# Attention and two expert mixtures on one core: the attention's transposed output in groups of 32 rows instead of 96

## The chip, the cores and the metric

The kernel runs on one core of one Trainium2 chip. The metric is the device time of one execution in microseconds (us). A core has five engines with queues of their own: TensorE (PE, with PEld for its weight loads), VectorE (DVE), ScalarE (ACT), GpSimd (POOL) and SyncE (SP), which issues most of the DMAs. All data are computed in float32; a matmul of float32 operands shows in the trace as two passes, each with a weight load (LDWEIGHTS) and a MATMUL record.

## The reference

Three stages follow one another. First a linear attention with decay over 4 batches, 8 heads, 768 positions and 48 dimensions a head:

```python
for t in range(S):
    cur = np.einsum('bhd,bhe->bhde', u[None] * kt, vt)
    y[:, :, t] = np.einsum('bhd,bhde->bhe', rt, state + cur)
    state = wt[:, :, :, None] * state + np.einsum('bhd,bhe->bhde', kt, vt)
```

Its output, heads side by side, is x with 3072 tokens and 384 columns. The first mixture computes h = x @ w_in (384 x 1024), h times its softmax, a layer norm with the gains g_ln, and the product with w_out (1024 x 384). The second mixture takes for each token the expert with the largest logit x @ w_gate, out of 8, and computes gate * (relu(x @ w1[e]) @ w2[e]) with w1[e] of 384 x 1024.

## The kernel before, in words

The attention works on 24 units: 6 chunks of 128 positions times 4 batches. A unit's tensors r, k and w are transposed on TensorE (L693), two heads in one block of 128 rows (64 rows a head, 48 of them used), so that there are four pairs p = 0 to 3. Products of the decays turn r and k into `rt` and `kt`. `scores` (L763 to L768) multiplies them, head by head, into two PSUM banks (4 and 5), with 48 rows of the array from row 0 or from row 64 on. `mask` (L771, VectorE) puts the causal part into `am`, on whose diagonal GpSimd has laid the u term (L748).

`y` (L775 to L781) computes the unit's output already transposed, features on partitions and the 128 positions along the free axis, in bank 4. For pair p, the stationary operand of 96 columns is the state `St[b]` (for chunks after the first; moving operand `rt`), and then v of either head with zeros beside it (`lv` holds 48 columns of v and 48 zeros a head; moving operand `am`). So the bank gets four blocks of 96 rows by 128 positions, from 12 matmuls (8 in the first chunk), with all 128 columns of the array addressed or 96 of them.

The mixture wants three blocks of 128 features for its contraction. `high` (L784 to L788) therefore copies blocks 0 to 2 to rows 0 to 95 in one ScalarE copy (L785) and the fourth block's three thirds to rows 96 to 127 in three more of 32x128 (L787); `low` (L790 to L794) does the same on VectorE with the subtraction that leaves the low part of each number (L791, L793). The two parts are the operands of `moe_h`, which forms each float32 product from three cheaper ones (`mm3`, L183). Since the features then stand in an order of their own, w_in is loaded in that order too: `x_rows` (L217) names two slices of rows for each block, and `from_f64` loads each slice with a DMA of its own (L224 to L226).

Next on the same banks: U (L808 to L811), the product that updates the state, uses bank 4 from chunk steps in the mixture stage on, and the next unit's scores overwrite banks 4 and 5. So both wait for the last of L793.

The order of all work around this is written out by hand: each step is entered in a plan with a nominal time (`at`, tables `OFF`), the steps are sorted by it, and `_ORDER` gives the sequence in which they are issued (`emit`). Every engine works through its steps in that order. Units 0 to 6 run beside the preparation of w_out and w_in (float64 to float32 by bit operations on VectorE, L231 to L237), units 7 to 23 beside one tile each of the first mixture, seven units behind. After the last unit come the rest of the mixture and the experts. `warm` (L1084) issues products that nobody reads, where TensorE has no work early on.

Of the kernel before, what the change touches and what calls it, by code (L numbers as in the profile page):

```python
# [7 lines left out]
F32 = mybir.dt.float32  # L8
# [5 lines left out]
ALU = mybir.AluOpType  # L14
# [17 lines left out]
# Places by number of tokens, in the order in which they are worked on, and the room of each; the last one's rest has a path of its own.  # L32
# [5 lines left out]
# Issue order: position in the issue sequence -> index of the step in the plan sorted by nominal time.  # L38
# [82 lines left out]
def rwkv_moe_kernel(ctx: ExitStack, tc: tile.TileContext, r, k, v, w, u, w_in, w_out, g_ln, w_gate, w1, w2, out, dbg=None):  # L121
# [44 lines left out]
    # sums of the inverse decay products, of the squares of the first mixture, of the decay products: bounds that NaN fails too  # L166
# [16 lines left out]
    def mm3(o, terms):  # L183
        """The products of operands in two parts each, high parts first; the product of both low ones is below float32."""
        n = len(terms)
        for i, (ah, al, bh, bl) in enumerate(terms):
            nc.tensor.matmul(o, ah, bh, start=(i == 0), stop=False)  # L187
            nc.tensor.matmul(o, ah, bl, start=False, stop=False)  # L188
        for i, (ah, al, bh, bl) in enumerate(terms):
            nc.tensor.matmul(o, al, bh, start=False, stop=(i == n - 1))  # L190

    def mm3_steps(o, terms, n):
        """The same in pieces of n products."""
        seq = [(ah, b) for ah, al, bh, bl in terms for b in (bh, bl)] + [(al, bh) for ah, al, bh, bl in terms]
        for i, (a, b) in enumerate(seq):
            nc.tensor.matmul(o, a, b, start=(i == 0), stop=(i == len(seq) - 1))  # L196
            if i % n == n - 1:
                yield
# [5 lines left out]
    # A plan is a list of steps with nominal times; every engine issues its steps in that order.  # L204
# [11 lines left out]
    # The rows of a block of the attention's transpose: those of a pair of heads, and a third of the last pair's.  # L216
    def x_rows(kk):  # L217
        return (slice(0, 96), slice(96 * kk, 96 * kk + 96)), (slice(96, 128), slice(3 * 96 + 32 * kk, 3 * 96 + 32 * kk + 32))

    def from_f64(src, n, pool, ck=None):  # L220
        """float64 to float32 by its bits: sign and exponent and 20 bits of the high word, 3 of the low one.
        Below float32's range it is 0, or, with ck, sums there say that a value was below."""
# [21 lines left out]
    def prep_w_in(c, pool, ck=None):  # L244
        kk, n = divmod(c, 2)
        ns = slice(512 * n, 512 * n + 512)
        a = yield from from_f64([(rows, w_in[at, ns]) for rows, at in x_rows(kk)], 512, pool, ck)
        yield lambda: nc.scalar.copy(out=wih[:, kk, ns], in_=a)
        yield lambda: nc.gpsimd.tensor_tensor(out=wil[:, kk, ns], in0=a, in1=wih[:, kk, ns].bitcast(F32), op=ALU.subtract)
# [7 lines left out]
    def prep_gate(f, st, wgt, pool, tp, gp):  # L257
        """Rows of w_out times the gate's weights, for the logits to come out of the same product as the mixture."""
        def tr():
            for kk in range(KD):  # L260
                nc.tensor.transpose(tp[:, kk, :], st()[:, kk * 128:(kk + 1) * 128], ident)
        yield tr
        wT = pool("wT")[:, 0:DM].rearrange("p (k n) -> p k n", k=KD)
        yield lambda: nc.scalar.copy(out=wT, in_=tp)

        def lg():
            for kk in range(KD):
                nc.tensor.matmul(gp[:, f, :], wT[:, kk, :], wgt[:, kk, :], start=(kk == 0), stop=(kk == KD - 1))
        yield lg
# [43 lines left out]
    def moe_act(u, halves, mw):  # L313
        """halves: the hidden values, as one pattern or as two of one bank each."""
# [121 lines left out]
    def experts_loop(x2d=None, tokd=None):  # L436
        """Every expert over all tokens, the others' results dropped; without those over its sorted rows."""
# [56 lines left out]
    def general_path():  # L494
# [44 lines left out]
        with ExitStack() as gs:  # L539
# [11 lines left out]
            with tc.For_i(0, NTOK, 128) as t0:  # L551
                x = ga2.tile([128, DM], F32, tag="gx", name="gx")
                xk = x.rearrange("p (k n) -> p k n", k=KD)
                nc.sync.dma_start(out=xk[:, :, 0:96], in_=xd[bass.ds(t0, 128), 0:288].rearrange("p (k n) -> p k n", k=KD))
                nc.sync.dma_start(out=xk[:, :, 96:128], in_=xd[bass.ds(t0, 128), 288:384].rearrange("p (k n) -> p k n", k=KD))
# [20 lines left out]
    # the attention's buffers go when its last tile is done, and those of the experts take their room  # L576
# [23 lines left out]
    def xslot(m):  # L600
        """Where the two parts of a tile's transpose wait: in the first weight buffers, as long as no expert has them; one place apart, for the last tile."""
        i = m % 7
        parts = [xs[:, 0], xs[:, 1]] if i == 2 else [t[:, DM * XPOS[i]:DM * XPOS[i] + DM] for t in wa0]
        return [t.rearrange("p (k n) -> p k n", k=KD) for t in parts]
# [12 lines left out]
    def lazy(t, make, gaps):  # L617
        """Steps of a generator that allocates as it goes: each is drawn when its turn comes."""
# [10 lines left out]
    # Nominal times of the steps of a unit from the start of its step: attention with the preparation of  # L629
    # w_out beside it, with that of w_in, with a tile of the mixture, and the mixture alone.  # L630
# [122 lines left out]
    def plan_A(i, t, mode):  # L753
# [5 lines left out]
        yp = bank[4][0:2 * D]  # L759
# [15 lines left out]
        def y():  # L775
            vf = v_.rearrange("p h d -> p (h d)")
            terms = [(p, St[b][:, p, :], u["rt"][:, p, :]) for p in range(4)] if c else []
            terms += [(p, vf[:, 96 * (2 * p + q) - 48 * q:96 * (2 * p + q) - 48 * q + 96], u["am"][:, q, p, :]) for q in range(2) for p in range(4)]
            for n, (p, a, m) in enumerate(terms):
                nc.tensor.matmul(yp[:, p, :], a, m, start=(n == 0), stop=(n == len(terms) - 1), skip_group_check=True)  # L780
# [3 lines left out]
        def high():  # L784
            nc.scalar.copy(out=xh[0:96], in_=yp[:, 0:3, :])  # L785
            for kk in range(KD):
                nc.scalar.copy(out=xh[96:128, kk, :], in_=yp[32 * kk:32 * kk + 32, 3, :])  # L787
        at(o("x"), high)  # L788

        def low():  # L790
            nc.vector.tensor_tensor(out=xl[0:96], in0=yp[:, 0:3, :], in1=xh[0:96].bitcast(F32), op=ALU.subtract)  # L791
            for kk in range(KD):
                nc.vector.tensor_tensor(out=xl[96:128, kk, :], in0=yp[32 * kk:32 * kk + 32, 3, :], in1=xh[96:128, kk, :].bitcast(F32), op=ALU.subtract)  # L793
# [57 lines left out]
    # groups of token tiles that are gated together  # L851
# [44 lines left out]
    def gate_steps(g, bk):  # L896
        """The first of the largest logits' experts, its gate, the row among the sorted tokens, and the way there."""
# [69 lines left out]
    # The first is the one with most of the first tokens, so that its work can start before the last tokens have theirs;  # L967
    # the others follow by their numbers of tokens, as PLACE has it. The j-th has room for SLOTS[j] tokens.
# [90 lines left out]
    # the first loads, then the constant buffers  # L1059
# [8 lines left out]
    def init():  # L1068
# [10 lines left out]
        # each partition's sums start at its share of the expert's first row: ranks come out as rows  # L1079
# [4 lines left out]
    def warm(n):  # L1084
        """The tensor engine's clock rises only under load: products that nobody reads, where there is no work yet."""
# [21 lines left out]
    def scratch(c):  # L1107
        """Where the preparation of a block of weights works: buffers that the mixture uses later."""
# [12 lines left out]
    def named(make, times):  # L1121
        """Steps of a generator at given times."""
# [80 lines left out]
    def check():  # L1203
        """1 for more tokens of the last place, 2 for a place with too little room, 4 for decays or values out of bounds or an expert's rows overrun."""
# [79 lines left out]
    # the first expert's first tokens, beside the end of the first mixture  # L1284
# [18 lines left out]
    # the order of the others  # L1303
# [18 lines left out]
    for j in range(1, NE):  # L1322
        # the weights and tokens of a place are made ready during the one before
# [72 lines left out]
```

## Time and profile before

| | |
|---|---|
| Median of 3 runs | 702.67 us (701.42, 703.84, 702.67) |
| Profiled execution, first to last instruction | 701.8 us |
| What lies around that span | not listed; the runs' median is 0.9 us above it |
| Granted TensorE clock, mean | 0.972 of full speed |
| TensorE, VectorE, ScalarE, GpSimd busy | 93%, 63%, 49%, 50% |
| DMA | 72.45 MB, mean 103 GB/s |

The execution has three parts: to about 101 us the attention's first units and the preparation of weights, to about 383 us attention and mixture together, and then the mixture's end and the experts. Busy shares of the whole span mix these, so the rows below are taken by part. Matmuls are pipelined: a record lasts longer than the engine's turn, so the time of a run of matmuls is read from the start of its first to the start of what follows.

### The profile page before, as it was taken

The page shows a single profiled execution, that of the slowest core. Times are in us where ns is not written, and L with a number is a line of the kernel's source. Part 1 is how long each engine was busy: PE and PEld are TensorE (multiplying, and loading weights), DVE is VectorE, ACT ScalarE, POOL GpSimd, SP SyncE. Part 2 cuts the span into 40 slices and gives each one's busy share as a digit, 9 for nine tenths or more (in the row PEclk, how much of TensorE's full clock was granted, in tenths as well). Part 3 has the DMA queues.
Part 4 walks back from the last instruction along what each step waited for, and adds up shares of the span by engine and source line. Part 5 has one row for each costly group of instructions (what it writes and reads, how often), then busy time and mean ns, then how long its engine had stood idle before and what let it go on. Part 6 is the DMA issues. An engine that isn't in the chain of part 4 may idle for free. (4 is left out here: it accounts for less than half of the span.)

```text
span 701.8 us, 11888 instructions
## 1 busy us (share of the span) xinstructions
PE 650.1 (93%) x4279; PEld 604.1 (86%) x4279; DVE 444.6 (63%) x947; ACT 346.1 (49%) x759; POOL 350.8 (50%) x341
## 2 busy tenths in 40 slices
PE   6787779898999999999989999999999999999993
PEld 6777668887988978998978998999899999999993
DVE  7999999968987888699887779752203121131220
ACT  3677566545553545545643556433535344353430
POOL 5666578344344445344461153326637374667721
PEclk9789799999999999999999999999999999999997
DMA  7856323562611413050200420155444253544400
GB/s 175 210 132 146 95 59 90 170 170 58 147 35 33 104 23 68 23 114 24 57 35 13 154 84 13 57 160 188 149 141 139 91 176 125 182 135 145 157 20 35
DMA packets 125193, 72.45 MB, mean 103 GB/s; under 512 B 104167, under 2 KB 115932, under 8 KB 125125
## 3 DMA queue, kind: packets, MB, share of 16 engines
q1 hardware_dynamic: 121845, 62.13, 33.3%
q0 software_dynamic: 3280, 9.47, 3.6%
q8 instruction: 36, 0.59, 0.4%
q14 instruction: 32, 0.26, 0.1%
HBM read 55.79 MB, written 16.29 MB: 103 GB/s over the span
## 5 line engine op out<-in xcount | busy, mean ns | idle before, releaser
L1257 DVE SCALAR_TENSOR_TENSOR hl<-bank,hh 128x384 fp32r<-128x384 f32 (+5 forms) x70 | 37.6, 552 | 141.4 <-ACT hh L1256 125.8
L1050 POOL TENSOR_TENSOR wbl<-stg,wbh 128x768 fp32r<-128x768 f32 x32 | 58.8, 1852 | 30.0 <-ACT wbh L1049 25.6
L196 PE MATMUL bank<-wbh,hh 128*128 128x384 f32 (+4 forms) x216 | 72.9, 338 | 0.0
L196 PE MATMUL bank<-wbl,hh 128*128 128x384 f32 (+4 forms) x216 | 72.6, 336 | 0.0
L187 PE MATMUL bank<-xth,wah 128*128 128x384 f32 (+5 forms) x210 | 71.2, 345 | 0.5 <-DVE rr L955 0.5
L1050 POOL TENSOR_TENSOR wal<-stg,wah 128x1024 fp32r<-128x1024 f32 x24 | 57.3, 2401 | 28.1 <-ACT wah L1049 28.1
L188 PE MATMUL bank<-xtl,wah 128*128 128x384 f32 (+5 forms) x210 | 69.7, 337 | 0.0
L187 PE MATMUL bank<-wbh,lh 128*128 128x392 f32 x192 | 67.5, 351 | 1.3 <-ACT xo L873 0.8
L1256 ACT ACTIVATE hh<-bank 128x384 fp32r<-128x384 f32 (+5 forms) x70 | 33.6, 490 | 66.6 <-PE bank L190 59.0
L188 PE MATMUL bank<-wbl,lh 128*128 128x392 f32 x192 | 65.5, 341 | 0.0
L748 POOL TENSOR_TENSOR am<-ident,a 128x1024 f32<-128x1024 f32 x24 | 46.7, 1946 | 28.0 <-DVE a L743 19.8
L1276 POOL DMA_INDIRECT out_dram<-yo,xg x28 | 27.6, 984 | 64.6 <-ACT yo L1273 42.7
L726 POOL TENSOR_TENSOR tq<-qe,yq 128x512 f32<-128x512 f32 x24 | 29.7, 1238 | 60.0 <-ACT yq L721 59.9
L780 PE MATMUL bank<-am,lv 128*96 128x128 f32 x384 | 49.3, 284 | 5.7 <-DVE am L771 4.8
L780 PEld LDWEIGHTS bank<-am,lv 128*96 128x96 f32 x384 | 45.9, 171 | 6.7 <-DVE am L771 3.2
L823 POOL TENSOR_TENSOR St<-su,qe 64x192 f32<-64x192 f32 x40 | 24.8, 621 | 48.0 <-DVE su L818 36.4
L190 PE MATMUL bank<-xth,wal 128*128 128x384 f32 (+5 forms) x210 | 48.2, 337 | 0.0
L961 POOL DMA_INDIRECT xsd<-xo,ai x24 | 25.4, 1057 | 35.0 <-DMA xsd<-xo,ai 14.1
L187 PE MATMUL pair<-wah,wah 128*128 128x512 f32 x102 | 42.1, 413 | 0.0
L196 PE MATMUL bank<-wbh,hl 128*128 128x384 f32 (+4 forms) x216 | 42.1, 336 | 0.0
L187 PEld LDWEIGHTS bank<-xth,wah 128*128 128x128 f32 x210 | 39.5, 188 | 2.3 <-DVE rr L955 0.7
L188 PEld LDWEIGHTS bank<-xtl,wah 128*128 128x128 f32 x210 | 39.5, 188 | 1.3
(241 smaller groups left out, 1753.0 us busy)
## 6 DMA issues: line engine op xcount, KB each, us to landing
stg<-in_moe_w_dram SPq DMA_DIRECT2D x32, 384.0 KB, 4.5
stg<-in_moe_w_dram SPq DMA_DIRECT2D x24, 512.0 KB, 4.5
xsd<-zrow SPq DMA_DIRECT2D x16, 386.0 KB, 3.8
xg<-xsd SPq DMA_DIRECT2D x24, 193.0 KB, 2.7
lw<-in_w_dram SPq DMA_DIRECT2D x24, 192.0 KB, 3.3
lr<-in_r_dram SPq DMA_DIRECT2D x24, 192.0 KB, 4.2
lk<-in_k_dram SPq DMA_DIRECT2D x24, 192.0 KB, 3.8
lv<-in_v_dram SPq DMA_DIRECT2D x24, 192.0 KB, 3.1
```

The costliest lines, as they stand in the source:

```text
L187: nc.tensor.matmul(o, ah, bh, start=(i == 0), stop=False)
L188: nc.tensor.matmul(o, ah, bl, start=False, stop=False)
L190: nc.tensor.matmul(o, al, bh, start=False, stop=(i == n - 1))
L196: nc.tensor.matmul(o, a, b, start=(i == 0), stop=(i == len(seq) - 1))
L726: nc.gpsimd.tensor_tensor(out=u["tq"], in0=u["qe"][:, :, 1:129], in1=u["yq"], op=ALU.mult)
L748: nc.gpsimd.tensor_tensor(out=u["am"].rearrange("p q a t -> p (q a) t"), in0=ident.rearrange("p (o t) -> p o t", o=1).to_broadcast([128, H ...
L780: nc.tensor.matmul(yp[:, p, :], a, m, start=(n == 0), stop=(n == len(terms) - 1), skip_group_check=True)
L961: nc.gpsimd.indirect_dma_start(out=xsd, out_offset=bass.IndirectOffsetOnAxis(ap=u["ai"][:, j, :], axis=0), in_=MU[m]["xo"], in_offset=None ...
L1050: at(t + c1, lambda: eng.tensor_tensor(out=dl(), in0=u["st"], in1=dh().bitcast(F32), op=ALU.subtract))
L1256: at(t + d1, lambda: nc.scalar.activation(out=P2["h", 0][:, f, cs], in_=hp, func=AF.Relu))
L1257: at(t + d2, lambda: nc.vector.scalar_tensor_tensor(out=P2["h", 1][:, f, cs], in0=hp, scalar=0.0, in1=P2["h", 0][:, f, cs].bitcast(F32), o ...
L1276: nc.gpsimd.indirect_dma_start(out=out, out_offset=bass.IndirectOffsetOnAxis(ap=xg(j, i)[0:n, XW - 1:XW].bitcast(I32), axis=0), in_=box["y ...
```

## The change

`y` writes the output as twelve groups of 32 rows, g = 3p + j with j = 0 to 2 the third of pair p, at rows 32 (g mod 4) of block g div 4. That is the natural order of the 384 features, three blocks of 128. Each group has its own matmuls with 32 stationary columns: one with the state, and one with v of the head that it lies in, or two for the middle third, which takes 16 rows from each head. That makes 28 matmuls (16 in the first chunk) instead of 12 (8). The copies are then one of 128x384 on ScalarE and one subtraction of 128x384 on VectorE, and w_in is loaded in plain blocks of 128 rows, with one DMA each. The general path, for inputs out of bounds, reads its rows with one DMA instead of two. The plan, its times and its order stay; comments are taken out.

```diff
-    def x_rows(kk):
-        return (slice(0, 96), slice(96 * kk, 96 * kk + 96)), (slice(96, 128), slice(3 * 96 + 32 * kk, 3 * 96 + 32 * kk + 32))
...
-        a = yield from from_f64([(rows, w_in[at, ns]) for rows, at in x_rows(kk)], 512, pool, ck)
+        a = yield from from_f64([(slice(0, 128), w_in[kk * 128:(kk + 1) * 128, ns])], 512, pool, ck)
...
-                xk = x.rearrange("p (k n) -> p k n", k=KD)
-                nc.sync.dma_start(out=xk[:, :, 0:96], in_=xd[bass.ds(t0, 128), 0:288].rearrange("p (k n) -> p k n", k=KD))
-                nc.sync.dma_start(out=xk[:, :, 96:128], in_=xd[bass.ds(t0, 128), 288:384].rearrange("p (k n) -> p k n", k=KD))
+                nc.sync.dma_start(out=x, in_=xd[bass.ds(t0, 128), :])
...
-        yp = bank[4][0:2 * D]
+        yp = bank[4]
...
         def y():
             vf = v_.rearrange("p h d -> p (h d)")
-            terms = [(p, St[b][:, p, :], u["rt"][:, p, :]) for p in range(4)] if c else []
-            terms += [(p, vf[:, 96 * (2 * p + q) - 48 * q:96 * (2 * p + q) - 48 * q + 96], u["am"][:, q, p, :]) for q in range(2) for p in range(4)]
-            for n, (p, a, m) in enumerate(terms):
-                nc.tensor.matmul(yp[:, p, :], a, m, start=(n == 0), stop=(n == len(terms) - 1), skip_group_check=True)
+            st = [(3 * p + j, St[b][:, p, 32 * j:32 * j + 32], u["rt"][:, p, :]) for p in range(4) for j in range(3)] if c else []
+            one = lambda j, q, off: [(3 * p + j, vf[:, 96 * (2 * p + q) + off:96 * (2 * p + q) + off + 32], u["am"][:, q, p, :]) for p in range(4)]
+            terms = st + one(0, 0, 0) + one(1, 0, 32) + one(1, 1, -16) + one(2, 1, 16)
+            begun = set()
+            for n, (g, a, m) in enumerate(terms):
+                kk, i = divmod(g, 4)
+                nc.tensor.matmul(yp[32 * i:32 * i + 32, kk, :], a, m, start=i not in begun, stop=n == len(terms) - 1, skip_group_check=True)
+                begun.add(i)
...
-        def high():
-            nc.scalar.copy(out=xh[0:96], in_=yp[:, 0:3, :])
-            for kk in range(KD):
-                nc.scalar.copy(out=xh[96:128, kk, :], in_=yp[32 * kk:32 * kk + 32, 3, :])
-        at(o("x"), high)
+        at(o("x"), lambda: nc.scalar.copy(out=xh, in_=yp[:, 0:KD, :]))
 
         def low():
-            nc.vector.tensor_tensor(out=xl[0:96], in0=yp[:, 0:3, :], in1=xh[0:96].bitcast(F32), op=ALU.subtract)
-            for kk in range(KD):
-                nc.vector.tensor_tensor(out=xl[96:128, kk, :], in0=yp[32 * kk:32 * kk + 32, 3, :], in1=xh[96:128, kk, :].bitcast(F32), op=ALU.subtract)
+            nc.vector.tensor_tensor(out=xl, in0=yp[:, 0:KD, :], in1=xh.bitcast(F32), op=ALU.subtract)
         at(o("x") + 0.9, low)
```

## Rows read from the trace of the kernel before

**Rows 1.** The page: busy us of each engine, share of the span, instructions.

```profile
PE 650.1 (93%) x4279; PEld 604.1 (86%) x4279; DVE 444.6 (63%) x947; ACT 346.1 (49%) x759; POOL 350.8 (50%) x341
```

**Rows 2.** Busy us by stretch: PE, PEld, DVE, ACT, POOL (instructions), clock, DMA.

```profile
20.00:101.00 81.00, 60.73 (x484) 56.52 (x484) 79.37 (x106) 53.51 (x131) 53.14 (x46) 0.84 0.50 120
101.00:383.00 282.00, 269.42 (x1890) 243.94 (x1888) 237.97 (x503) 145.68 (x344) 129.42 (x146) 1.00 0.31 75
383.00:700.00 317.00, 305.63 (x1765) 290.30 (x1764) 111.07 (x305) 137.83 (x267) 155.95 (x107) 0.99 0.38 120
```

**Rows 3.** TensorE's waits: total us, times, longest; before 101 us, then 101 to 383.

```profile
PE bank L767 <- DVE wal L793: 6.9, 3, 5.3
...
PE bank L780 <- DVE am L771: 4.0, 4, 1.9
...
PE bank L810 <- DVE wal L793: 0.9, 1, 0.9
```

**Rows 4.** Copies of one line: ns minimum/median/maximum, first and last start.

```profile
L787 ACT CAST wah<-bank x60: 253/255/258, 23.3 to 363.4; 32x128 fp32r<-32x128 f32 x60
...
L793 DVE TENSOR_TENSOR wal<-bank,wah x60: 282/286/291, 26.3 to 366.0; 32x128 fp32r<-32x128 f32 x60
...
L785 ACT CAST wah<-bank x20: 457/475/479, 22.9 to 362.4; 96x384 fp32r<-96x384 f32 x20
...
L791 DVE TENSOR_TENSOR wal<-bank,wah x20: 523/550/554, 25.7 to 364.9; 96x384 fp32r<-96x384 f32 x20
```

**Rows 5.** Timeline of VectorE from 20 us: start, us, instruction.

```profile
26.25 0.89 DVE L793 TENSOR_TENSOR wal<-bank,wah 32x128 fp32r<-32x128 f32 x3
27.17 1.49 DVE L231 TENSOR_SCALAR t<-stg 128x384 int32<-128x384 int32 x1
...
30.75 0.35 DVE L231 TENSOR_SCALAR t<-stg 128x384 int32<-128x384 int32 x1
```

**Rows 6.** Busy us by stretch of L793 (VectorE), then of L787 (ScalarE).

```profile
20.00:101.00 81.00, 5.16 (x18) 0.84 0.50 120
101.00:383.00 282.00, 15.47 (x54) 1.00 0.31 75
...
101.00:383.00 282.00, 13.80 (x54) 1.00 0.31 75
```

**Rows 7.** Busy us by stretch of L780, the output product: PE, PEld.

```profile
101.00:383.00 282.00, 47.93 (x408) 45.35 (x408) 1.00 0.31 75
```

**Rows 8.** Timeline of TensorE around one output product (start, us, instruction).

```profile
215.73 1.04 PE L780 MATMUL bank<-rt,St 128*96 128x128 f32 x8
216.60 1.91 PE L780 MATMUL bank<-am,lv 128*96 128x128 f32 x16
218.93 0.42 PE L187 MATMUL bank<-wbh,lh 128*128 128x392 f32 x1 [0.42 <-DVE lg L869]
```

**Rows 9.** The same around one unit's scores.

```profile
208.44 0.60 PE L693 MATMUL bank<-ident,lk 128*128 128x128 f32 x4
208.97 1.16 PE L767 MATMUL bank<-rt,kt 48*128 48x128 f32 x16
210.06 0.66 PE L693 MATMUL bank<-ident,lw 128*128 128x128 f32 x4
```

**Rows 10.** In flight within 20 to 40 ns from 209.29, 210.07 and 215.83 us.

```profile
208.97 0.60 PE L767 MATMUL bank<-rt,kt 48*128 48x128 f32 x6
...
209.85 0.28 PE L767 MATMUL bank<-rt,kt 48*128 48x128 f32 x2
...
215.73 0.38 PE L780 MATMUL bank<-rt,St 128*96 128x128 f32 x2
```

**Rows 11.** Timeline of TensorE: a run of idle-time products and what follows.

```profile
23.03 1.11 PE L1087 MATMUL pair<-ones 128*128 128x128 bf16 x17
23.98 0.61 PE L693 MATMUL bank<-ident,lr 128*128 128x128 f32 x4
```

**Rows 12.** SP's loads of the first mixture's input weights: ns, first and last start.

```profile
L226 SPq DMA_DIRECT2D stg<-in_moe_w_in_dram x12: 312/417/1222, 44.3 to 74.9; - x12
```

## The prediction

> **What bounds the kernel now.** I read the page's busy times first, then the busy times by stretch, then the waits, and only then the timeline around one product. TensorE is busy 93% of the span [rows 1], but that is an average over stages with different limits. The change touches nothing after the last tile's transpose is split, at 380 us, so two stretches matter [rows 2]. From 20 to 101 us (the first six attention units, with the weights' preparation beside them) VectorE is busy 79.4 of 81 us and TensorE 60.7: VectorE is the limit. From 101 to 383 us (17 more units, each with a tile of the first mixture) TensorE is busy 269.4 of 282 us and VectorE 238.0: TensorE is the limit, at 16.6 us a unit, with VectorE at 84% behind it. From 383 to 700 us nothing of the change runs. The waits say the same: before 101 us TensorE waits for VectorE, the longest for the last small subtraction of L793 (the next scores want its bank); after 101 us TensorE hardly waits, and only 0.9 us of it for L793 [rows 3].
>
> **The small copies.** A unit loses three ScalarE copies of 32x128 (255 ns each) and three VectorE subtractions of 32x128 (286 ns); the two large ones go from 96x384 to 128x384 [rows 4]. The rows show no charge for partitions: other instructions of this kernel differ in elements per partition, and 384 stay 384, so I keep 475 and 550 ns. Bounds for the large pair: nothing, or a third more (0.16 + 0.18 us a unit); I take nothing. A triple on VectorE takes 0.89 us of its queue [rows 5].
> Before 101 us that is 18 subtractions, 5.16 us of VectorE [rows 6], plus a seventh unit just behind that edge, 0.86: 6.0 us off the engine that sets the time. Not all comes back. A preparation step of one shape, L231, takes 1.49 us once and 0.35 another time [rows 5]; such instructions wait inside for something that VectorE's own queue does not show, and pulling them forward does not shorten that. I take 5 of 6.0, with bounds of 2 and 8: the higher one because the scores that L793 holds up [rows 3] also get 0.77 us of ScalarE's copies less in front of them.
> After 101 us the 15.5 us of VectorE and 13.8 of ScalarE [rows 6] lie beside TensorE and cost nothing themselves. What they can give there is the waits that end in L793, 0.9 us, and a part of the 4.0 us in which the output product waits for the masks [rows 3]. I take 1.
>
> **The product.** One unit's product is 12 matmuls before (4 with the state, 8 with the scores), and each shows as two passes: 24 records, 408 in 17 units [rows 7]. Eight of them start in 215.73 to 216.60 us, 109 ns apart [rows 8]; 24 take 2.61 us. After, there are 28 matmuls, 56 passes over the same 128 moving columns. One behind another that would be 6.1 us. So everything hangs on whether matmuls whose outputs stand in different groups of 32 rows run side by side. No row has such a case. The nearest are the scores, where two matmuls use different rows of the array (48 rows from 0 and from 64): 16 passes start within 208.97 to 210.06 us, 68 ns apart on average instead of 109 [rows 9], and a stretch of 20 ns finds six of them in flight, against two of the output product [rows 10]. So two small matmuls do share the array. I take the same for four groups of columns. The order of the 28 helps: each four, counted from the first, fall in four different groups. That makes 7 rounds of two passes, 14 x 109 ns = 1.53 us.
> Sharing has a price at both ends. The four transposes ahead of the scores hold the engine from 208.44 to 208.97, 0.53 us, where four passes at 109 ns are 0.44; and the scores take 1.09 us where 8 pairs at 109 ns are 0.87 [rows 9]. Together 0.3 us a switch, which the output product, full width today, does not pay. The Trainium skill (TensorEngine Tiling (Array Packing), Key Properties) says that changing the tiling mode drains the engine; the trace agrees, with the 0.3 us just found, and by its rule alone the product would cost that much more than the rounds. New total 1.85 us (1.53 + 0.31); the unit gains 0.76, and 17 units 12.9 us of TensorE.
> The other resource is issue: 56 loads and 56 matmuls in 1.85 us. The densest run before is 17 idle-time products with a load each in 23.03 to 23.98 us, 56 ns a pair [rows 11], which is the array's time there and so only an upper bound. At that pace the unit costs 56 x 56 = 3.1 + 0.3 = 3.4 us, 0.8 more than today; at full overlap 1.85. I take the full overlap, because the scores' pairs start close enough for six to be in flight, and keep 3.4 for the range.
> How much of 12.9 us reaches the end? VectorE goes from 14.0 to 13.1 us a unit (238.0 / 17, less 0.86) and stays behind TensorE (269.4 / 17 = 15.8, less 0.76), but the issue order is fixed, and each of the waits of [rows 3] after 101 us can grow when TensorE arrives sooner. I take 80%, 10 us; bounds 6 and 13.
> Before 101 us the product is not the limit: 4 units have 16 passes, now 32, and TensorE has 20 us of room. Cost nothing; without that cover the loss in the serial case is below.
>
> **Weights and the rest.** The weights of the first mixture come in six loads of 512 KB instead of twelve; six issues go from SP's queue at a median of 417 ns [rows 12], 2.5 us of a queue. VectorE, which consumes them, is busy all through [rows 2], which hides it: I take 0, bounds 0 and -2.5. The same bytes move. The general path's load stands in a branch that doesn't run.
>
> **Sum.** -5 (VectorE early) - 10 (TensorE late) - 1 (waits) = -16. The profiled span is 701.8 us and the runs' median 702.67, 0.9 above it; 701.8 - 16 + 0.9 = 686.7 us. With the bounds of the terms: -2 - 6 = -8 at the least, -8 - 13 - 2 = -23 at the most, so 680 to 695.
>
> **Rivals.**
> (1) Slower: passes block in program order. If the second pass of a matmul, which must wait for the first in its own column group, holds back everything behind it, only neighbours overlap: second pass of one with first pass of the next. 28 matmuls then need 29 turns of 109 ns, 3.16 + 0.31 = 3.5 us, 0.9 more than today; 17 units give +15, less 5 and 1: 712 us. The pace of 56 ns a pair from above comes out beside it (3.4). It decides as soon as a product takes over 2.6 us. For it: the scores' 1.09 us fit nine turns, with one pass alone first and one alone last, as well as eight pairs and a longer switch. Against it: late in the scores, at 210.07 to 210.11 us, the last two passes are still both in flight, and nothing else of theirs [rows 10]; in blocked order the last would be alone. The Trainium skill (TensorE: Matmul & The Clock Gate, "The mechanism" under Part 3) has matmuls start and end in strict program order without reordering; applied to both passes of one product this is that rival, and the last pair speaks against it only if the passes were listed one matmul after another.
> (2) Slower, much: no sharing between column groups. 56 x 109 = 6.1 us, 3.5 more; 17 units give +60. Early units pay 1.7 us more each, inside TensorE's 20 us of room. 702.7 + 60 - 5 = 758 us. It is also the case in which the change doesn't do what its shapes suggest. For it: no row shows column groups at work, and sharing by rows gives each stream its own partitions, while four column groups read the same 128 partitions at once. Against: [rows 10].
> (3) The gain is there but swallowed: the mixture's chain on VectorE takes TensorE's place at once, and the early preparation waits inside as before. Then -2 early and -2 late: 699 us. For it: VectorE at 84%. Against: it gets lighter by 0.86 us a unit itself.
>
> **How the numbers follow.** Forecast 0.60 (range of its own 680 to 695); rival (1) 0.17; rival (2) 0.14; rival (3) 0.09, of which two thirds are over 0.3% (2.1 us, about what runs of this kernel can tell from no change). Faster: 0.60 + 0.06 = 0.66, taken as 0.65; same: 0.03, and 0.01 of rival (1) from a product of just today's length, 0.04; slower: 0.31. The range runs from 680 to 714: it takes in the forecast, (3) and (1), and leaves out (2) and a part of the tails.
>
> **What the profile after would show.** The output product's 56 records in about 1.8 us, eight of them in flight at a time; 3.4 us would be rival (1) or the issue pace, 6 us rival (2). The stretch of a mixture unit at 15.9 to 16.0 us instead of 16.6; the seventh unit's end some 5 us sooner; no 32x128 copies. [...] The forecast is wrong if a product takes over 2.6 us, or if TensorE's waits for VectorE after 101 us grow by over 7 us.

## The result, and the profile after

The changed kernel takes 687.03 us (median; 686.02 to 687.3) against 702.83 us before: 0.9774 of the time, 95% interval 0.9760 to 0.9787. The forecast was 686.7 us. Its total is right and one of its two large terms is not: the experiments below show that the time behind 101 us came mostly from the copies, which the prediction gave nothing there, and less than half of it from TensorE.

The page and the busy times by stretch, to set beside [rows 1, 2]. The stretches end at other times now, since the mixture begins at 94 us instead of 100 and the attention ends near 360 instead of 380.

```profile
PE 637.4 (93%) x4983; PEld 582.4 (85%) x4983; DVE 417.5 (61%) x875; ACT 325.1 (48%) x687; POOL 351.8 (51%) x341
```

```profile
20.00:94.00 74.00, 60.06 (x645) 52.65 (x644) 68.84 (x88) 47.70 (x112) 51.66 (x44) 0.75 0.51 128
94.00:360.00 266.00, 250.50 (x2412) 220.45 (x2409) 218.93 (x438) 127.84 (x286) 130.13 (x144) 0.99 0.32 80
360.00:684.00 324.00, 311.44 (x1791) 295.09 (x1790) 114.07 (x318) 140.50 (x274) 157.83 (x112) 0.99 0.36 117
```

VectorE was busy for 98% of the first stretch and is now busy for 93%; the second one has TensorE at 94% and VectorE at 82%, nearly as before. It is 15.6 us a unit (266 us for 17), where the prediction had 15.9 to 16.0.

The copies and the loads, as in [rows 4, 12]: one of each where four and two stood, and 128 partitions take what 96 took (479 against 475 ns, 546 against 550).

```profile
L784 ACT CAST wah<-bank x20: 460/479/500, 24.2 to 345.2; 128x384 fp32r<-128x384 f32 x20
...
L787 DVE TENSOR_TENSOR wal<-bank,wah x20: 525/546/558, 25.1 to 347.1; 128x384 fp32r<-128x384 f32 x20
...
L222 SPq DMA_DIRECT2D stg<-in_moe_w_in_dram x6: 340/341/521, 42.5 to 70.2; - x6
```

The product in the timeline of TensorE, as in [rows 8], and below it what is in flight within 10 and 20 ns from 190.70 and 190.90 us, as in [rows 10]. The 56 passes and the way out of them hold the engine from 190.51 to 192.18 us, 1.67 us where 24 passes took 2.61; a moment finds eight and then twelve passes in flight instead of two. Four column groups do run side by side: 14 turns of 109 ns are 1.53 us.

```profile
190.51 0.86 PE L779 MATMUL bank<-rt,St 128*32 128x128 f32 x24
191.19 1.06 PE L779 MATMUL bank<-am,lv 128*32 128x128 f32 x32
192.18 0.66 PE L687 MATMUL bank<-ident,lk 128*128 128x128 f32 x4
```

```profile
190.51 0.42 PE L779 MATMUL bank<-rt,St 128*32 128x128 f32 x8
...
190.64 0.51 PE L779 MATMUL bank<-rt,St 128*32 128x128 f32 x12
```

To see where the time went I use two marks that every run has: the start of the first mixture's first matmul (it ends the stretch that VectorE bounds) and the start of the last unit's scores. Between them lie the units that run beside the mixture. Before the change, in the timeline of TensorE:

```profile
99.96 0.77 PE L187 MATMUL pair<-wah,wah 128*128 128x512 f32 x1
...
367.76 1.16 PE L767 MATMUL bank<-rt,kt 48*128 48x128 f32 x16
```

and after:

```profile
94.02 0.80 PE L187 MATMUL pair<-wah,wah 128*128 128x512 f32 x1
...
350.80 1.16 PE L761 MATMUL bank<-rt,kt 48*128 48x128 f32 x16
```

So 5.9 us came before the first mark, 11.0 between the two (267.8 to 256.8 us), and the rest of the program added half a microsecond. (This pair of profiled executions differs by 17.5 us, the medians by 15.8.) The marks come from one execution of each kernel, so differences between them are rough: e2 and e4 below have products of the same length and medians 0.4 us apart, and yet differ by 2.5 us between the marks. All runs, with the same marks read from their traces:

| run | median, us | ratio to before (95%) | first mark | between the marks |
|---|---|---|---|---|
| before | 702.8 | | 99.96 | 267.8 |
| after | 687.0 | 0.9774 (0.9760 to 0.9787) | 94.02 | 256.8 |
| e1 new product, old copies | 700.0 | 0.9958 (0.9940 to 0.9977) | 99.20 | 264.8 |
| e5 new copies, product as long as the old | 691.6 | 0.9849 (0.9832 to 0.9865) | 94.47 | 261.2 |
| e2 product's scores part in pairs | 689.5 | 0.9793 (0.9759 to 0.9827) | 95.46 | 258.7 |
| e4 product in pairs | 689.9 | 0.9799 (0.9765 to 0.9834) | 95.45 | 261.2 |
| e3 product group by group | 733.8 | 1.0424 (1.0388 to 1.0459) | 99.60 | 295.7 |
| e6 VectorE in four | 697.7 | 0.9927 (0.9906 to 0.9949) | 99.50 | 261.6 |
| e7 ScalarE in four | 688.1 | 0.9795 (0.9778 to 0.9811) | 93.90 | 258.0 |
| e8 VectorE loaded elsewhere | 723.2 | 1.0298 (1.0281 to 1.0315) | 100.94 | 283.1 |
| e9 centring on ScalarE | 696.2 | 0.9908 (0.9881 to 0.9935) | 93.51 | 266.6 |
| e12 VectorE unloaded elsewhere | 679.1 | 0.9665 (0.9648 to 0.9682) | 93.81 | 250.4 |
| e10 two loads again | 687.1 | 0.9779 (0.9752 to 0.9806) | 94.08 | 256.3 |
| e11 state update in groups | 686.7 | 0.9775 (0.9738 to 0.9812) | 94.09 | 256.9 |

### The profile page after: what moved, and what is told of

It reads as the page before. It is cut to its first block, busy times and chain, and to the rows that moved or that the text cites. A ratio compares the mean times of both kernels' runs of the same rounds, so it can differ in the third digit from the quotient of the medians.

```text
span 684.3 us, 13116 instructions
## 1 busy us (share of the span) xinstructions
PE 637.4 (93%) x4983; PEld 582.4 (85%) x4983; DVE 417.5 (61%) x875; ACT 325.1 (48%) x687; POOL 351.8 (51%) x341
## 5 line engine op out<-in xcount | busy, mean ns | idle before, releaser
L187 PEld LDWEIGHTS bank<-xth,wah 128*128 128x128 f32 x210 | 39.5, 188 | 2.7 <-DVE rr L949 0.7
L765 DVE COPY_PREDICATED am<-causal,bank 128x512 f32<-128x512 int32 x48 | 34.2, 737 | 12.4 <-PE bank L761 7.8
L188 PEld LDWEIGHTS bank<-xtl,wah 128*128 128x128 f32 x210 | 39.5, 188 | 1.3
L188 PE MATMUL pair<-wal,wah 128*128 128x512 f32 x102 | 40.6, 398 | 0.0
```

What stands on the lines that cost most here:

```text
L765: nc.vector.copy_predicated(out=u["am"][:, q], mask=causal.bitcast(I32).rearrange("p (o t) -> p o t", o=1).to_broadcast([128, 4, 128]), da ...
```

## The experiments

Each starts from the changed kernel.

**e1: the product alone.**

```diff
-        at(o("x"), lambda: nc.scalar.copy(out=xh, in_=yp[:, 0:KD, :]))
+            nc.scalar.copy(out=xh[0:96], in_=yp[0:96, 0:KD, :])
+            for kk in range(KD):
+                nc.scalar.copy(out=xh[96:128, kk, :], in_=yp[96:128, kk, :])
...
-            nc.vector.tensor_tensor(out=xl, in0=yp[:, 0:KD, :], in1=xh.bitcast(F32), op=ALU.subtract)
+            nc.vector.tensor_tensor(out=xl[0:96], in0=yp[0:96, 0:KD, :], in1=xh[0:96].bitcast(F32), op=ALU.subtract)
+            for kk in range(KD):
+                nc.vector.tensor_tensor(out=xl[96:128, kk, :], in0=yp[96:128, kk, :], in1=xh[96:128, kk, :].bitcast(F32), op=ALU.subtract)
```

> The new product with the old pattern of copies: one of 96x384 and three of 32x128 on ScalarE, and the same on VectorE; result unchanged. Theory (the product's four column groups run side by side and give the time from 101 us on, the copies give it before): the product stays at 1.67 us, the lead over the kernel before is about 0 at 101 us and 10 to 11 us at the end, 691 to 693 us. Rival (the time comes from the copies, which shorten the chain and VectorE's queue everywhere): 700 us or more.

Measured: 700.0 us, so the theory falls. The product is as short as in the change (198.08 to 199.75 us below), 0.9 us less in each of the 16 products that lie between the marks, 15 us together, and yet only 3.0 us are gained there. The first two fences are e1's timeline of TensorE at one product and at the marks, the third its longest waits between them.

```profile
198.08 0.86 PE L779 MATMUL bank<-rt,St 128*32 128x128 f32 x24
198.76 1.06 PE L779 MATMUL bank<-am,lv 128*32 128x128 f32 x32
199.75 0.44 PE L687 MATMUL bank<-ident,lk 128*128 128x128 f32 x2
...
99.20 0.50 PE L187 MATMUL pair<-wah,wah 128*128 128x512 f32 x1
...
364.00 1.16 PE L761 MATMUL bank<-rt,kt 48*128 48x128 f32 x16
```

```profile
PE bank L779 <- DVE am L765: 4.9, 5, 2.2
PE bank L384 <- DVE cc L359: 2.0, 2, 1.3
PE bank L810 <- DVE wal L793: 1.9, 3, 0.8
PE bank L938 <- DVE oh L919: 1.8, 1, 1.8
PE bank L187 <- ACT xo L873: 1.8, 1, 1.8
```

All of TensorE's listed waits between the marks add up to 21.2 us here, against 12.3 before the change: over half of what the product saves, TensorE now waits, and four of the five longest are for VectorE. The prediction had named waits for VectorE that grow by over 7 us as a sign of being wrong; those between the marks are 11.5 us before the change, 18.6 in e1 and 13.0 in the change, so the sign shows only where the copies stay old.

**e5: the copies alone.** The same question from the other side.

```diff
             terms = st + one(0, 0, 0) + one(1, 0, 32) + one(1, 1, -16) + one(2, 1, 16)
+            terms += [(i, vf[:, 192 * p + 48:192 * p + 80], u["am"][:, 0, p, :]) for p in range(4) for i in range(4)]
```

> The change with 16 more matmuls a product that add zeros (the zero columns beside v as stationary operand), so that the product lasts about as long as before the change (2.5 us instead of 1.67; its result is the same). It is the copies' share by itself. Theory Q (VectorE's queue binds before and after 101 us, TensorE hardly): 690 to 692 us, the product's share in the change 3 to 5 us. Theory of the prediction (after 101 us TensorE binds): 696 to 698 us.

Measured: 691.6 us, inside the range of theory Q. The product lasts 2.54 us again (190.83 to 193.37).

```profile
190.83 0.86 PE L780 MATMUL bank<-rt,St 128*32 128x128 f32 x24
191.51 1.93 PE L780 MATMUL bank<-am,lv 128*32 128x128 f32 x64
193.37 0.44 PE L687 MATMUL bank<-ident,lk 128*128 128x128 f32 x2
...
94.47 0.50 PE L187 MATMUL pair<-wah,wah 128*128 128x512 f32 x1
...
355.70 1.16 PE L761 MATMUL bank<-rt,kt 48*128 48x128 f32 x16
```

With e1, before and after this gives four cells between the marks: 267.8 with neither, 264.8 with the product alone, 261.2 with the copies alone, 256.8 with both. The product is worth 3.0 us (old copies) or 4.4 us (new ones), the copies 6.6 or 8.0. The medians of the whole runs agree in the main: 2.9 us with the product alone, 11.4 with the copies alone, 15.8 with both. Ahead of the first mark the copies give 5.5 us by themselves, the product 0.8.

**e2, e4, e3: the order of the matmuls within a product.** e2 and e4 let two column groups alternate, in the scores' part or in both; e3 sorts by group.

```diff
+            def pairs(ts):
+                by = [[x for x in ts if x[0] % 4 == i] for i in range(4)]
+                return [x for a in (0, 2) for two in zip(by[a], by[a + 1]) for x in two]
-            terms = st + one(0, 0, 0) + one(1, 0, 32) + one(1, 1, -16) + one(2, 1, 16)
+            terms = st + pairs(one(0, 0, 0) + one(1, 0, 32) + one(1, 1, -16) + one(2, 1, 16))  # e2
+            terms = pairs(st) + pairs(one(0, 0, 0) + one(1, 0, 32) + one(1, 1, -16) + one(2, 1, 16))  # e4
+            terms.sort(key=lambda x: x[0] % 4)  # e3, after the line of the change
```

> The new copies, with the products of the scores ordered so that only two column groups alternate (groups 0 and 1 first, then 2 and 3); the state's part as in the change. The product should then last about as long as before the change: 6 + 16 turns of 109 ns and the switch, 2.7 us. Theory: lead of 5 to 6 us at 101 us, only 1 more behind it, 695 to 697 us. Rival (copies give it all): 687 us. If the order of issue within a product doesn't matter, since each column group has a queue of its own: product 1.7 us and 687 us too, told apart from the rival by the product's length.

> The change with its matmuls ordered so that two column groups alternate at a time (0 and 1, then 2 and 3), in the state's part and in the scores'. Theory: 28 turns of 109 ns and the switch, 3.3 us a product, 1.5 more than the change: 17 units give +26, 713 us. If order means nothing: 687 us.

> The change with its 28 matmuls sorted by column group, all seven of one group before the next. If matmuls of one group follow one another and nothing passes them: 56 turns of 109 ns and the switch, 6.4 us a product, 4.5 more than the change in each of 17 units: 763 us, up to 768 with the early units. If each column group works from its own queue: 1.7 us and 687 us. If the gain was the copies' alone and the order means nothing: 687 us.

Measured: 689.5, 689.9 and 733.8 us. None of these expectations was met in size. The product took 2.13 us in e2 and in e4 and 5.01 in e3, where 2.7, 3.3 and 6.4 were expected; e2 is therefore no test of the copies, e5 is. The order does count, but less than I had assumed: here is e3's product from 206.31 us on, group 0's seven matmuls being issued before any of group 1's.

```profile
206.31 0.84 PE L780 MATMUL bank<-rt,St 128*32 128x128 f32 x6
206.98 0.71 PE L780 MATMUL bank<-am,lv 128*32 128x128 f32 x5
207.43 0.30 PE L780 MATMUL bank<-rt,St 128*32 128x128 f32 x1
207.53 0.27 PE L780 MATMUL bank<-am,lv 128*32 128x128 f32 x1
207.56 0.27 PE L780 MATMUL bank<-rt,St 128*32 128x128 f32 x1
207.64 0.27 PE L780 MATMUL bank<-am,lv 128*32 128x128 f32 x1
207.67 0.27 PE L780 MATMUL bank<-rt,St 128*32 128x128 f32 x1
207.75 0.27 PE L780 MATMUL bank<-am,lv 128*32 128x128 f32 x1
```

The am passes are group 0's (five and three of its eight), the St passes from 207.43 us on are group 1's, later in the program: they start while three passes of group 0 have not started. A column group's passes thus run ahead of another's by a few, and e3 needs 44 turns of 109 ns instead of 56 (5.01 less the 0.2 of the way out). As a price list: 3.34 us more product a unit cost 38.9 us between the marks (0.73 per microsecond of the 16 products), 0.87 more (e5) cost 4.4 (0.32).

**e6, e7: which engine's copies.** The two halves of e1's edit, each alone.

> The change with VectorE's subtraction in four again (96x384 and three of 32x128), ScalarE's copy in one. Theory Q: nearly all of the copies' gain goes, 698 to 700 us. Theory L (it is the time from the product's end to the free bank that counts, for U and the next scores; ScalarE's three copies and VectorE's three weigh about the same in it): 693 to 694 us.

> The change with ScalarE's copy in four again, VectorE's subtraction in one. Theory Q: 687 to 689 us, since ScalarE is half idle. Theory L: 693 to 694 us.

Measured: 697.7 and 688.1 us, as theory Q has it (e6 0.3 us short of its range). VectorE's three subtractions cost 10.7 us, ScalarE's three copies 1.1 (the intervals of e7 and the change overlap), though both stand in the same chain behind the product and take nearly the same time. Of e6's loss 4.8 us lie between the marks, 0.32 for each microsecond of VectorE there (17 triples of 0.87), 5.5 ahead of the first and the rest behind the second. e6 at the marks:

```profile
99.50 0.80 PE L187 MATMUL pair<-wah,wah 128*128 128x512 f32 x1
...
361.11 1.16 PE L761 MATMUL bank<-rt,kt 48*128 48x128 f32 x16
```

Theory L doesn't fall by this alone, because its premise that both weigh about the same does not hold. One unit of the change, whose passes with v (`am`, `lv`) start at 191.19 us (shown above), and the same unit of e7 show it: ScalarE's copies take 0.6 us longer, and in both VectorE's subtraction starts 3.13 us behind the first of these passes, since VectorE comes to it later than the copies end.

```profile
192.46 0.49 ACT L784 CAST wah<-bank 128x384 fp32r<-128x384 f32 x1
194.32 0.55 DVE L787 TENSOR_TENSOR wal<-bank,wah 128x384 fp32r<-128x384 f32 x1
```

```profile
191.76 1.06 PE L779 MATMUL bank<-am,lv 128*32 128x128 f32 x32
193.03 0.48 ACT L785 CAST wah<-bank 96x384 fp32r<-96x384 f32 x1
193.51 0.59 ACT L787 CAST wah<-bank 32x128 fp32r<-32x128 f32 x3
194.89 0.55 DVE L791 TENSOR_TENSOR wal<-bank,wah 128x384 fp32r<-128x384 f32 x1
```

Over the 16 units between the marks the time from the start of the last pass with v to the end of the last subtraction is 3.95 us in the mean in the change, 4.73 in e6 and 4.17 in e7. So e6 and e7 show that it is VectorE's copies that cost, and leave open whether they cost by VectorE's queue or by the later free bank.

**e8: VectorE loaded in another place.**

```diff
             nc.vector.tensor_reduce(out=u["a0"].rearrange("p q a -> p a q"), in_=u["ru"].rearrange("p (a q) d -> p a q d", q=2), axis=AX.X, op=ALU.add)
+            for _ in range(3):
+                nc.vector.tensor_tensor(out=ap0_junk[0:32], in0=onesf[0:32], in1=ident[0:32], op=ALU.subtract)
```

> The change with three small VectorE subtractions of constants, 32x128, whose results nobody reads, put behind the reduction of the u term (a0), where they delay neither the bank's release nor the x operands directly. Theory Q: as slow as three small subtractions behind the product, in proportion to what they take of VectorE (0.6 to 0.9 us a unit): 696 to 700 us. Theory L: 687 to 689 us.

Measured: 723.2 us. The direction is theory Q's, the size is off, because the load was: the instructions take 280 ns in the median but up to 1978, and 52.8 us in all (2.2 us a unit instead of 0.6 to 0.9). The row gives minimum, median and maximum, and below it stands the second of one unit's three beside GpSimd.

```profile
L740 DVE TENSOR_TENSOR ap_junk<-onesf,ident x72: 268/280/1978, 9.6 to 378.3; 32x128 f32<-32x128 f32 x72
...
155.90 1.90 POOL L745 TENSOR_TENSOR am<-ident,a 128x1024 f32<-128x1024 f32 x1 [0.62 <-DVE a L738]
155.97 1.97 DVE L740 TENSOR_TENSOR ap_junk<-onesf,ident 32x128 f32<-32x128 f32 x1
```

The trace shows what they wait for. Of the 72, 30 took over 0.3 us; each of these started while a GpSimd instruction with two operands ran, and ended 0.14 us after it. None of the 42 short ones started beside one. Here GpSimd ends at 157.80 us and the subtraction at 157.94. The place was an unlucky choice: a0, just ahead, is what GpSimd's product for `am` waits for. Other VectorE instructions got shorter in exchange, and VectorE's busy time rose by 37.3 us (454.8 against 417.5 in the change). The granted clock between the marks is also lower, 0.95 against 0.99, so the 36.2 us that e8 lost are no clean price for load on VectorE.

**e9: VectorE unloaded onto ScalarE.**

```diff
-            nc.vector.tensor_scalar(out=u["cc"], in0=u["s"], scalar1=u["nmu"], scalar2=None, op0=ALU.add)
+            if cen_act:  # the 17 units beside the attention
+                nc.scalar.activation(out=u["cc"], in_=u["s"], func=AF.Identity, bias=u["nmu"])
+            else:
+                nc.vector.tensor_scalar(out=u["cc"], in0=u["s"], scalar1=u["nmu"], scalar2=None, op0=ALU.add)
```

> The change with the mixture's centring (cc = s - mean, 128x1024, 0.90 us of VectorE a unit) on ScalarE (about 1.1 us there) for the 17 units beside the attention; nothing else changed, and nothing near the product or its copies. Theory Q (VectorE's queue binds): at the half microsecond of time per microsecond of VectorE that the three small subtractions showed, 17 x 0.9 x 0.5 = 8 us faster than the change, 678 to 681 us. If TensorE binds after the change: 686 to 687 us. If ScalarE's later squares hold the chain: 689 us or more.

Measured: 696.2 us, 9 us slower than the change, against theory Q and in the range of the third case. VectorE's busy time between the marks falls as meant (211.2 to 196.2 us), but its own listed waits rise from 39.5 to 64.2 us, and ScalarE's instruction of 1149 ns waits for VectorE's mean, 25.2 us in total, with ScalarE's later work behind it.

```profile
L360 ACT ACTIVATE cc<-s,nmu x17: 1133/1149/1156, 104.3 to 366.3; 128x1024 f32<-128x1024 f32 x17
...
  DVE nmu L357: 25.2, 11
...
  PEld bank L387: 5.5, 5
  PE bank L387: 4.2, 2
```

So VectorE's queue is not the bound in the sense that any relief of it pays: where the relief holds another engine's queue, it costs. e12 takes load off VectorE without putting it anywhere.

**e12: VectorE unloaded.** The refinement of the mixture's 1/sqrt(var) is left out.

```diff
-            nc.vector.scalar_tensor_tensor(out=sm("tt"), in0=u["y0"], scalar=u["var"], in1=u["y0"], op0=ALU.mult, op1=ALU.mult)
-            nc.vector.tensor_scalar(out=u["tt"], in0=u["tt"], scalar1=-0.5, scalar2=1.5, op0=ALU.mult, op1=ALU.add)
-            nc.vector.tensor_tensor(out=sm("rstd"), in0=u["tt"], in1=u["y0"], op=ALU.mult)
+            u["rstd"] = u["y0"]
```

> The change without the three VectorE instructions that refine the mixture's 1/sqrt(var) once more (L376 to L378; that part of the computation is left out). They are 13.8 us of VectorE in the 16 units up to 360 us, 0.86 a unit, as much as three small subtractions, away from the product and its copies, and nothing is put on another engine. Theory Q (any microsecond off VectorE's queue beside the attention gives about half of one): 679 to 682 us. Theory C (the small subtractions count for their place, ahead of the steps that wait for the product's bank, and VectorE's load elsewhere doesn't): 686 to 687 us.

Measured: 679.1 us, 8.0 less than the change; theory C falls. 6.4 us of it lie between the marks, 0.46 for each microsecond of the instructions left out. VectorE's busy time there fell by 9.0 us only (211.2 to 202.2), since others got longer; by that it is 0.71. e12 also shortens chains: in the change ScalarE waits 4.8 us for the refined value, and the time from the last pass with v to the end of the subtraction falls from 3.95 to 3.47 us. So VectorE's work away from the product counts too; whether by its queue or by these chains, e12 doesn't tell.

```profile
93.81 0.79 PE L187 MATMUL pair<-wah,wah 128*128 128x512 f32 x1
...
344.20 1.16 PE L759 MATMUL bank<-rt,kt 48*128 48x128 f32 x16
```

**e10, e11.** The loads split again (twelve issues), and the state update's product cut to the used blocks.

```diff
-[(slice(0, 128), w_in[kk * 128:(kk + 1) * 128, ns])]
+[(slice(0, 96), w_in[kk * 128:kk * 128 + 96, ns]), (slice(96, 128), w_in[kk * 128 + 96:(kk + 1) * 128, ns])]  # e10
...
-                nc.tensor.matmul(up[:, p, :].rearrange("p (q d) -> p q d", q=2), u["ks"][:, p, :], v_[:, 2 * p:2 * p + 2, 0:D], start=True, stop=True)
+                for q in range(2):  # e11
+                    nc.tensor.matmul(up[64 * q:64 * q + 64, p, 48 * q:48 * q + 48], u["ks"][:, p, 64 * q:64 * q + 64], v_[:, 2 * p + q, 0:D], start=True, stop=True)
```

> The change with each of the six loads of w_in split into rows 0 to 95 and 96 to 127 again, twelve issues as before the change. The prediction's step (SP's six issues less are hidden): 687 us, within 1. If they counted: 689 to 690 us.

> The change with the state update's product also cut to the blocks that are used: 8 matmuls of 64 columns in two column groups with 48 moving columns, instead of 4 of 128 columns with 96. TensorE would need 0.45 us and 0.3 for the switch instead of 0.92 in 13 of the units beside the mixture. Theory Q: TensorE's time counts little, 686 to 687 us. If TensorE binds after the change: 684 to 685 us.

Measured: 687.1 and 686.7 us, both the change's time. The six issues were hidden. e11's product holds TensorE for 0.61 us (198.33 to 198.94), where the change's takes 0.86 (198.09 to 198.95), and nothing comes of it: too small a step to tell much at 0.3 a microsecond, and no version that beats the change.

## Why the prediction was right, and where it was not

- *Column groups side by side, 1.85 us a product.* Right; 1.67 us. Rivals (1) and (2), 712 and 758 us, fall with it: no product beside the mixture took over 2.6 us. The switch was priced a little high (0.3 us, against 0.14 behind the rounds and 0.09 ahead of them).
- *VectorE early, -5 of 6.0 us.* Right in place and size: the first mark comes 5.9 us sooner, 5.5 with the copies alone (e5), and back to 99.50 with VectorE's subtractions alone (e6).
- *TensorE late, -10.* This is the step that failed: 12.9 us of TensorE at 80%. Its size was a little low (0.94 us a unit instead of 0.76), its share far too high: of 15 us between the marks it gave 3.0 alone and 4.4 on top of the copies, so 20 to 30%. The bounds of 6 to 13 did not hold it.
- *Copies late, "lie beside TensorE and cost nothing themselves", -1.* The same error seen from VectorE: 6.6 to 8.0 us. The two errors cancel, and 16 came out as 15.8. That the total was right is luck, and no proof of its parts.
- The reading behind both: TensorE busy 269 of 282 us [rows 2] was taken for the limit, VectorE at 84% for slack. Passes start 109 ns apart and each shows as a record of 273 ns in the median, so a busy 95% hides short gaps; in e1 TensorE's waits rose by nearly 9 us when its work fell by 15. Nor do idle shares tell which engine pays: after the change VectorE's listed waits between the marks (39.5 us) are longer than TensorE's (14.8), and yet a microsecond off VectorE returned more. With the order fixed on every engine, each stands idle while the work for it is held up on another. Rival (3) had the swallowed gain nearly right for the product alone (2 us late against 3.0), but gave the copies nothing beyond that. Whether the new copies helped the product's gain through (4.4 against 3.0 us) is less than these marks can tell.
- *A step that "waits inside".* Right as a reading: the 1.49 us of [rows 5], from 27.17 us on, end 0.22 us after GpSimd's `am` product, which ran from 26.55 to 28.44 us.
- *The range.* It leaves out two bounds that the text itself gives, -2.5 for the loads and a third more for the large copies. Neither was needed: the loads changed nothing (e10), and the large copies take what they took.
- *Loads, 0.* Right (e10).

What stays open: through which waits a microsecond of VectorE turns into a third to two thirds of one beside the mixture. e9 shows that the place in the other queues matters. In e6, e8 and e12 VectorE's load and the time from the last pass with v to the end of its subtraction moved together (4.73, 4.37 and 3.47 us against 3.95), so no run here parts VectorE's queue from the chain to the free bank.

## What to carry to other kernels

Where two engines with fixed orders are both over 80% busy, price a saving on either by what a microsecond there returns, not by which one is busier: here 0.2 to 0.3 saved on TensorE at 95%, and roughly 0.3 to 0.7 on VectorE at 84%. Try each half of such a change alone, even if the total came out as forecast. Small matmuls whose outputs stand in different groups of 32 rows can be cut up at a gain, if consecutive ones fall in different groups (1.67 us a product against 5.01 in the worst order); what that gains the kernel is another question, here 2.9 us by itself.

## What the runs showed of the hardware that was not expected

- Passes of one column group overtake earlier ones of another (e3: group 1 starts at 207.43 us, before group 0's last three). The Trainium skill (TensorE: Matmul & The Clock Gate, "The mechanism" under Part 3) has matmuls start in strict program order; between column groups this trace differs, and the measurement decides. No record says which pass of its matmul it is, but where the groups rotate, as in the change, all 24 passes with the state start ahead of the 32 with v, in the program's order. The same run ahead shortens e4 to 2.13 us where alternating pairs alone would need 28 turns, 3.05 us.
- A subtraction of 32x128 on VectorE takes 282 to 291 ns with one operand in PSUM [rows 4], and 17 of the 72 ran beside a GpSimd instruction with two operands. With both operands in SBUF it takes 268 to 1978 ns, 733 in the mean, and whenever it starts beside such an instruction it ends 0.14 us after it (e8, 30 of 72). A cheap instruction put in as a load can be the dearest on its engine.
